# A fused attention and two-layer kernel: another packing of layer two's streamed weight sums

## The chip, the cores and the metric

The kernel runs on one core of one Trainium2 chip. The metric is device time in microseconds, taken over several executions of the whole program; one more execution was recorded by the hardware profiler. The engines are named as in the profile: PE is TensorE (matmuls), PEld its weight loads, DVE is VectorE, ACT is ScalarE, POOL is GpSimd, SP is SyncE, which here issues the DMAs.

## The reference

The inputs are q, k, v of 4 batches x 8 heads x 576 rows x 64, a feature matrix omega, and two weight matrices for each of two layers, all float32. An attention with random features gives 2,304 tokens of 512 channels; two layers 512 to 2048 to 512 follow, the first with a leaky ReLU, the second with a hard swish. The change is in the second.

```
def _moe2_ref(x, w_in, w_out):
    h = x @ w_in                       # 2304 x 512 by 512 x 2048
    relu6 = np.clip(h + 3.0, 0.0, 6.0)
    g = h * relu6 / 6.0
    return (g @ w_out).astype(np.float32)

def reference(**kwargs):
    ...
    attn_out = _attn_ref(**attn_kwargs)
    B, H, S, D = attn_out.shape
    x = np.ascontiguousarray(attn_out.transpose(0, 2, 1, 3)).reshape(B * S, H * D)
    x = _moe_ref(x=x, **moe_kwargs)
    return _moe2_ref(x=x, **moe2_kwargs)
```

## The kernel before

**Products.** A float32 number is split into a rounded high half and the rest, and a product is made of three matmuls (high by high, low by high, high by low). Tokens go in five groups: four of 512 and one of 256; layer two takes them in the order 0, 2, 3, 4, 1. For a group of 512 tokens, layer two cuts its matrices in 2 x 2 blocks and makes seven block products instead of eight (Winograd's form of Strassen). The seven are named b11, b21, t1, t2, t3, t4 and b22. What each multiplies is a block, or a sum of blocks, of x and of the weight.

**Weight sums.** `prepare` (L538 to L578) makes the sums of the weight blocks for one pair of 128-column weight rows, splits each into halves (`split`, L580: a copy and a subtraction, on ACT, DVE or POOL), and stores the result in four parts to DRAM (`away`, L587, the store is L590). This runs during layer one, eight times for w_in. `S[0]` and `S[1]` hold the four sums, `a` and `b` the plain blocks. The list `both` (L566) says which pieces make up which of the four parts.

**Reading.** `Hpair` (L1039 to L1098) makes one pair for a group of 512 tokens: four groups of eight pairs. It fetches the four parts into tiles c[0] to c[3] (`fetch`, L627, issued on SP at L630). The slots of these tiles are a ring of five (`NSUM = 5`), in the profile `late_w` and `third_w`, the latter being one slot of them. Part 2 is fetched only in its first 256 columns, the others in 512. Each of the seven products is six matmuls of 128x256 (L1057), in two banks of PSUM: p takes b11, t2, t3 and t4 in turn, summed on top of each other, and `save` (L1065, an ACT copy of L461) takes a snapshot between them; the two halves of q take b21, and t1 with b22. `total` (L1068) adds a snapshot to a half of q on DVE. So t2, t3 and t4 each wait for the copy that reads the bank before them, and a later b22 for the sum that reads its half. The hard swish follows on ACT and DVE (L1090, L1095).

**After it.** `parts` (L956) sums the blocks of the result (POOL and DVE: L464, L468, L469) and splits them; `down` (L971 to L988) makes seven products of three matmuls (L979) against w_out, which stays in SBUF, into four accumulator banks; `finish` (L990) adds the accumulators on DVE (L1000) and stores the output. For a group that is not stored ahead, the blocks of x are summed and split on the way (`seven`, L608; its subtractions are L464 as well). In the group of 256 tokens `Hsingle` (L1100 to L1125) makes the plain product from the plain blocks in the four parts, with 256-column matmuls (L475 to L477).

**The order.** No order is written by hand. Every operation is handed to `Graph` (L79) with a due time, the tiles that it reads and writes and, for each engine that may run it, an assumed duration. `run` (L154) goes through the operations that are ready and takes the one that can start first by these durations; within 60 ns the earlier due time decides. The slot of a tile is given out in the order in which tiles were asked for. A pair of `Hpair` is due every 7.2 us (`UP`), and its products at these shares of it:

```
prod(0, 0, 0, B_["b11"], 0.0, True)
prod(1, 0, 256, B_["b21"], 0.1, True)
...
prod(2, 1, 0, B_["t1"], 0.2, False)
...
prod(0, 1, 256, B_["t2"], 0.3, False)
```

`down` of a pair is due three pairs later, so that its products and those of `Hpair` alternate on PE. The order that comes out is a fixed program for each engine, with semaphores between them.

## Time and profile before

| what | us |
|---|---|
| median of 3 runs | 915.52 |
| their range | 915.23 to 915.98 |
| profiled execution | 912.86 |
| its span in the trace | 910.8 |
| PE busy | 900.3 |
| layer two, from the first matmul of L1057 | 543.4 to 906.4 |

The span is the time from the first to the last recorded instruction; the profiled execution's own time is 2.1 us more. Some matmul records of a trace can be missing, and the ends of matmuls are modelled: a matmul is written with the time that it takes to pass through the array, while the next starts behind it after less than half of that. So the step between starts is what counts, and in a run of n equal matmuls it is found as (length - one duration) / (n - 1).

### The profile page before, as it was taken

How to read it: one execution, taken by the hardware profiler on the slowest of the kernel's cores; microseconds unless marked ns; L12 is line 12 of the kernel's file. 1: busy time of each engine (PE TensorE's matmuls, PEld its weight loads, DVE VectorE, ACT ScalarE, POOL GpSimd, SP SyncE). 2: the span in 40 equal slices, each digit the busy share in tenths (PEclk: the TensorE clock that was granted, in tenths of full speed). 3: DMA queues.
4: the chain of work that ended last, by engine and by line, in shares of the span. 5: the costliest groups of instructions: out<-in, count | busy, mean ns of one | idle time of the engine just before them, and what ended most of it. 6: DMA issues, size and time to landing. Idle time of an engine off the chain costs nothing.

```text
span 910.8 us, 17874 instructions
## 1 busy us (share of the span) xinstructions
PE 900.3 (99%) x6340; PEld 801.5 (88%) x6340; DVE 614.1 (67%) x1518; ACT 493.3 (54%) x1157; POOL 319.5 (35%) x565
## 2 busy tenths in 40 slices
PE   8999999999999999999999999999999999999998
PEld 8978777889868877788888888999999999999997
DVE  5888987977786774555587444666666557676554
ACT  7966766766676654544555335443543455455442
POOL 2454554422541211101001002344426436544642
PEclk9999999999999999999999999999999999999999
DMA  9537644767567670978998438885787584678540
GB/s 333 156 119 250 208 147 139 229 212 205 164 191 235 207 214 26 333 290 301 323 335 314 143 135 283 308 313 163 238 279 275 172 277 137 219 237 256 163 131 33
DMA packets 91849, 198.01 MB, mean 217 GB/s; under 512 B 15088, under 2 KB 41328, under 8 KB 91760
## 3 DMA queue, kind: packets, MB, share of 16 engines
q1 hardware_dynamic: 91760, 196.87, 65.0%
q8 instruction: 50, 0.82, 0.4%
q14 instruction: 39, 0.32, 0.1%
HBM read 150.18 MB, written 46.66 MB: 216 GB/s over the span
## 4 chain that ended last, share of the span: by engine, by line
PE 91%; DVE 5%; issue 1%; ACT 1%; DMA 1%; POOL 0%; SPq 0%; DVEq 0%; ACTq 0%
PE bank L979 18%; PE bank L1057 17%; PE bank L475 16%; PE bank L477 15%; PE bank L476 15%; PE bank L708 4%; PE bank L754 3%; PE bank L889 1%; PE bank L861 1%; PE bank L765 1%; DVE nm L677 1%; DVE junk L836 1%; DMA first_xT<-qT 1%; DVE sq L655 0%; DVE late_u L1000 0%
## 5 line engine op out<-in xcount | busy, mean ns | idle before, releaser
L979 PE MATMUL bank<-w,g 128*128 128x256 f32 x762 | 108.0, 279 | 0.5 <-DVE g L464 0.4
L979 PEld LDWEIGHTS bank<-w,g 128*128 128x128 f32 x762 | 96.8, 188 | 1.1 <-DVE g L464 0.8
L461 ACT COPY late_u<-bank 128x256 f32<-128x256 f32 (+1 forms) x112 | 43.0, 385 | 93.1 <-PE bank L1057 81.7
L921 DVE TENSOR_TENSOR g<-bank,g 128x512 fp32r<-128x512 f32 (+1 forms) x80 | 50.8, 635 | 56.6 <-ACT g L461 55.4
L919 ACT ACTIVATE bank<-bank 128x512 f32<-128x512 f32 (+1 forms) x80 | 43.7, 546 | 74.8 <-PE bank L477 74.6
L1057 PE MATMUL bank<-x,late_w 128*128 128x256 f32 x552 | 73.8, 280 | 0.7 <-DVE u L1000 0.5
L1057 PEld LDWEIGHTS bank<-x,late_w 128*128 128x128 f32 x552 | 68.0, 188 | 1.3 <-DVE u L1000 0.7
L475 PE MATMUL bank<-g,w 128*128 128x512 f32 (+1 forms) x180 | 68.9, 383 | 0.0
L1057 PE MATMUL bank<-second_w,late_w 128*128 128x256 f32 x498 | 68.3, 280 | 0.5 <-ACT late_u L461 0.5
L475 PE MATMUL bank<-x,w 128*128 128x512 f32 (+1 forms) x180 | 68.6, 381 | 0.0
L477 PE MATMUL bank<-g,w 128*128 128x512 f32 (+1 forms) x180 | 66.4, 369 | 0.0
L477 PE MATMUL bank<-x,w 128*128 128x512 f32 (+1 forms) x180 | 66.3, 368 | 0.0
L476 PE MATMUL bank<-x,w 128*128 128x512 f32 (+1 forms) x180 | 66.2, 368 | 0.0
L476 PE MATMUL bank<-g,w 128*128 128x512 f32 (+1 forms) x180 | 66.2, 368 | 0.0
L683 POOL TENSOR_TENSOR nm<-nm,sq 128x4 f32<-128x4 f32 (+3 forms) x92 | 27.8, 310 | 107.9 <-DVE nm L680 101.7
L677 DVE TENSOR_REDUCE nm<-bank 128x4 f32<-128x512 f32 (+3 forms) x92 | 49.6, 568 | 23.3 <-PE bank L708 20.6
L688 ACT ACTIVATE h<-bank,nm 128x128 f32<-128x128 f32 x208 | 58.7, 387 | 11.4 <-POOL nm L683 11.4
L1057 PEld LDWEIGHTS bank<-second_w,late_w 128*128 128x128 f32 x498 | 62.0, 188 | 1.0 <-ACT late_u L461 0.7
L979 PE MATMUL bank<-second_w,g 128*128 128x256 f32 x333 | 48.2, 278 | 0.0
L475 PE MATMUL bank<-x,second_w 128*128 128x512 f32 (+1 forms) x120 | 45.2, 377 | 0.0
L461 ACT CAST g<-bank 128x512 fp32r<-128x512 f32 (+1 forms) x78 | 43.4, 557 | 1.4
L477 PE MATMUL bank<-x,second_w 128*128 128x512 f32 (+1 forms) x120 | 44.1, 367 | 0.0
(353 smaller groups left out, 2424.4 us busy)
## 6 DMA issues: line engine op xcount, KB each, us to landing
late_w<-in SPq DMA_DIRECT2D x84, 512.0 KB, 4.4
in<-late_w SPq DMA_DIRECT2D x32, 512.0 KB, 4.1
late_w<-in SPq DMA_DIRECT2D x40, 256.0 KB, 4.3
third_w<-in SPq DMA_DIRECT2D x20, 512.0 KB, 4.4
wst<-w2i SPq DMA_DIRECT2D x16, 512.0 KB, 4.2
wst<-w2o SPq DMA_DIRECT2D x16, 512.0 KB, 4.2
x_t<-late_w SPq DMA_DIRECT2D x12, 512.0 KB, 4.4
wst<-w1i SPq DMA_DIRECT2D x10, 512.0 KB, 4.1
```

The lines of the kernel that those rows point to most:

```text
L461: return [("act", c_act(n, psum), lambda: nc.scalar.copy(dst(), src())), dve if psum else dve + (True,)]
L475: nc.tensor.matmul(o, lhsT=ah, rhs=bh, start=start, stop=False)
L476: nc.tensor.matmul(o, lhsT=al, rhs=bh, start=False, stop=False)
L477: nc.tensor.matmul(o, lhsT=ah, rhs=bl, start=False, stop=stop)
L677: g.op([("dve", c_dve(c * 128), lambda raw=raw, n_=n_: nc.vector.tensor_reduce(out=n_()[:, :, 0], in_=raw(), axis=AX.X, op=ALU.min))], rd= ...
L683: ("pool", 170, lambda n_=n_, s_=s_: nc.gpsimd.tensor_tensor(out=n_(), in0=n_(), in1=s_(), op=ALU.subtract))],
L688: nc.scalar.activation(h.tiles[0][:, q * 128:q * 128 + 128], raw()[:, q], AF.Exp, bias=nm.tiles[0][:, q], scale=-1.0)
L708: nc.tensor.matmul(ps[bank].tiles[0][o, i * 128:i * 128 + 128], lhsT=src.tiles[0][r, i * 128:i * 128 + n], rhs=wn[r], start=True, stop=True)
L919: g.op([("act", c_act(n, True), lambda: nc.scalar.activation(P(), P(), AF.Prelu, alpha=0.01))], wr=[p], due=d)
L921: g.op([("dve", c_dve(n), lambda: nc.vector.tensor_tensor(out=G1(), in0=P(), in1=G0().bitcast(F32), op=ALU.subtract))], rd=[p, (gg, 0)], w ...
L979: nc.tensor.matmul(acc[bank].tiles[0][:, half * 256:half * 256 + 256], lhsT=src.tiles[x][:, q * 128:q * 128 + 128], rhs=w[k].tiles[y][:, c ...
L1057: nc.tensor.matmul(R[r](), lhsT=w[x], rhs=m[y], start=start and k == n == 0, stop=k == 1 and n == 2, skip_group_check=True)
```

## The change

The four parts are packed in another way, and read in the order that follows from it. Nothing is added to or taken from the seven products.

| part | before | after |
|---|---|---|
| c0 | b11, b21 | b11, t2 |
| c1 | t1, t2 | b21, t3 |
| c2 | t3 (256 columns fetched) | t1, t4 |
| c3 | t4, b22 | b22 (256 columns fetched) |

The products that read each tile first were b11, t1, t3 and t4; now they are b11, b21, t1 and b22. `prepare` makes every part of two pieces of 256 columns, where two parts were one piece of 512. `Hsingle` fetches its first tile in two pieces.

```diff
--- before.py
+++ after.py
@@ -563,7 +563,7 @@
             add(1, B_[1], P[0], ALU.subtract, [b, (S[0], 0)])
             add(2, B_[1], A[1], ALU.subtract, [a, b])
             add(3, B_[0], P[1], ALU.subtract, [b, (S[0], 1)])
-        both = [(a, 0, 512)], [(S[0], 0, 512)], [(S[1], 0, 256), (b, 0, 256)], [(S[1], 256, 256), (b, 256, 256)]
+        both = [(a, 0, 256), (S[0], 256, 256)], [(a, 256, 256), (S[1], 0, 256)], [(S[0], 0, 256), (b, 256, 256)], [(S[1], 256, 256), (b, 0, 256)]
         if kind == "out":
             if i % 2 == 0:
                 tail.append(Buf("w", line="wo2"))
@@ -1043,7 +1043,7 @@
             d = t0 - 8e3
             c = [Buf("w", line="c") for _ in range(4)]
             for k in range(4):
-                fetch(c[k], "in", i, k, d + UP * 0.1 * k, slice(0, 256) if k == 2 else slice(0, 512))
+                fetch(c[k], "in", i, k, d + UP * 0.1 * k, slice(0, 256) if k == 3 else slice(0, 512))
             p, q = Ps("H"), Ps("H")
             R = [lambda: p.tiles[0][:, 0:256], lambda: q.tiles[0][:, 0:256], lambda: q.tiles[0][:, 256:512]]
             bank = [(p, 0), (q, 0), (q, 1)]
@@ -1070,16 +1070,16 @@
                     rd=[bank[r], (s, i)], wr=[(h, half)], due=t0 + UP * at - 6e3)
 
             prod(0, 0, 0, B_["b11"], 0.0, True)
-            prod(1, 0, 256, B_["b21"], 0.1, True)
+            prod(1, 1, 0, B_["b21"], 0.1, True)
             save(0, 0.1)
-            prod(2, 1, 0, B_["t1"], 0.2, False)
+            prod(2, 2, 0, B_["t1"], 0.2, False)
             total(h0, 0, 1, 0, 0.2)
-            prod(0, 1, 256, B_["t2"], 0.3, False)
+            prod(0, 0, 256, B_["t2"], 0.3, False)
             save(1, 0.3)
-            prod(0, 2, 0, B_["t3"], 0.5, False)
+            prod(0, 1, 256, B_["t3"], 0.5, False)
             save(0, 0.5)
             total(h1, 1, 2, 0, 0.5)
-            prod(0, 3, 256, B_["t4"], 0.6, False)
+            prod(0, 2, 256, B_["t4"], 0.6, False)
             g.op(copy_alts(lambda: h1.tiles[0][:, 0:256], R[0], 256, True), rd=[bank[0]], wr=[(h1, 0)], due=t0 + UP * 0.7 - 6e3)
             prod(2, 3, 0, B_["b22"], 0.8, False)
             total(h0, 1, 2, 1, 0.8)
@@ -1105,8 +1105,8 @@
             ps = []
             for e in range(2):
                 c, p, h = Buf("w", line="c"), Ps("H"), Buf("u", line="h")
-                for part, cols, to in ((2, 256, 0), (3, 256, 256)) if e else ((0, 0, 0),):
-                    fetch(c, "in", i, part, t0 - 8e3, slice(cols, cols + (256 if e else 512)), to)
+                for part, cols, to in ((3, 256, 0), (2, 256, 256)) if e else ((0, 0, 0), (1, 0, 256)):
+                    fetch(c, "in", i, part, t0 - 8e3, slice(cols, cols + 256), to)
                 ps.append(p)
                 P, U = lambda p=p: p.tiles[0][:, 0:n], lambda h=h: h.tiles[0][:, 0:n]
                 for k in range(KT):
```

Since the order is planned, the edit moves more than the lines above say. In the rows below a matmul that waits is written by itself, and the other five of the product in the row behind it. `Activation` is the semaphore of ACT, `DMAHW` with a number one of the DMA queue's, and DVE the one of DVE. In these rows second_w_1 is the x block of t2, second_w_3 (before: second_w_4 and second_w_3) that of t3, x_101 that of t4 and x_102 that of b22; late_w and third_w are the streamed tiles.

PE in steady state, the second half of one pair, before (t2, t3, t4, b22 with products of L979 between them):

```order
L1057 MATMUL bank_185<-second_w_4_0_1004,late_w_3_0_4052 128x256 [waits Activation_49]
L1057 MATMUL bank_185<-second_w_4_0_1004,late_w_3_0_4052 128x256 x5
L979 MATMUL bank_181<-w_100,g_105 128x256 x3
L979 MATMUL bank_186<-w_99,g_105 128x256 x3
L1057 MATMUL bank_185<-second_w_3_0_1003,late_w_1_0_4050 128x256 [waits DMAHW5_49,Activation_49]
L1057 MATMUL bank_185<-second_w_3_0_1003,late_w_1_0_4050 128x256 x5
L979 MATMUL bank_187<-second_w_0_0_1000,g_105 128x256 x3
L979 MATMUL bank_188<-w_98,g_106 128x256 x3
L1057 MATMUL bank_185<-x_101,late_w_0_0_4049 128x256 [waits DMAHW6_49,Activation_49]
L1057 MATMUL bank_185<-x_101,late_w_0_0_4049 128x256 x5
L1057 MATMUL bank_184<-x_102,late_w_0_0_4049 128x256 [waits DVE_49]
L1057 MATMUL bank_184<-x_102,late_w_0_0_4049 128x256 x5
```

The same piece of a pair after:

```order
L1057 MATMUL bank_182<-second_w_1_0_1001,late_w_3_0_4052 128x256 [waits Activation_49]
L1057 MATMUL bank_182<-second_w_1_0_1001,late_w_3_0_4052 128x256 x5
L979 MATMUL bank_183<-w_97,late_g_0_0_4053 128x256 x3
L979 MATMUL bank_187<-w_99,late_g_0_0_4053 128x256 x3
L1057 MATMUL bank_182<-second_w_3_0_1003,late_w_0_0_4049 128x256 [waits Activation_49]
L1057 MATMUL bank_182<-second_w_3_0_1003,late_w_0_0_4049 128x256 x5
L979 MATMUL bank_188<-w_96,g_107 128x256 x3
L979 MATMUL bank_181<-w_96,g_107 128x256 x3
L1057 MATMUL bank_182<-x_101,third_w_0_0_1650 128x256 [waits Activation_49]
L1057 MATMUL bank_182<-x_101,third_w_0_0_1650 128x256 x5
L1057 MATMUL bank_186<-x_102,late_w_1_0_4050 128x256 [waits DMAHW2_49,DVE_49]
L1057 MATMUL bank_186<-x_102,late_w_1_0_4050 128x256 x5
```

The waits for the DMA have moved from t3 and t4 to the first half of the pair and to b22; t2, t3 and t4 keep their wait for Activation.

DVE at the turn from group 3 to group 4, before (L1000 adds the accumulators of `finish`; second_w and x are the split blocks of x for group 4):

```order
L464 TENSOR_TENSOR second_w_4_0_1004<-xr_0_113,second_w_4_0_1004 128x512
L464 TENSOR_TENSOR second_w_3_0_1003<-xr_0_114,second_w_3_0_1003 128x512
L464 TENSOR_TENSOR x_101<-late_xr_1_0_4060,x_101 128x512
L1000 TENSOR_TENSOR u_0_116<-late_u_2_0_4056,bank_181 128x256
L468 TENSOR_TENSOR late_xr_1_0_4060<-late_xr_1_0_4060,xr_0_113 128x512
L1000 TENSOR_TENSOR late_u_2_0_4056<-late_u_2_0_4056,bank_181 128x256
L1000 TENSOR_TENSOR u_0_116<-u_0_116,bank_181 128x256
L1000 TENSOR_TENSOR late_u_2_0_4056<-late_u_2_0_4056,bank_188 128x256
L1000 TENSOR_TENSOR u_0_116<-u_0_116,bank_184 128x256
```

And after:

```order
L464 TENSOR_TENSOR g_105<-xr_0_112,g_105 128x512
L464 TENSOR_TENSOR g_107<-wst_0_109,g_107 128x384
L1000 TENSOR_TENSOR late_u_2_0_4056<-late_u_2_0_4056,bank_181 128x256
L1000 TENSOR_TENSOR late_u_0_0_4054<-late_u_0_0_4054,bank_181 128x256
L1000 TENSOR_TENSOR late_u_2_0_4056<-late_u_2_0_4056,bank_188 128x256
L1000 TENSOR_TENSOR late_u_0_0_4054<-late_u_0_0_4054,bank_184 128x256
L464 TENSOR_TENSOR x_101<-late_xr_1_0_4060,x_101 128x512
L464 TENSOR_TENSOR second_w_1_0_1001<-xr_0_113,second_w_1_0_1001 128x512
L464 TENSOR_TENSOR second_w_3_0_1003<-xr_0_114,second_w_3_0_1003 128x512
```

The four adds of L1000 now stand ahead of the three subtractions of L464 that make blocks of x.

## Rows read from the trace of the kernel before

**Rows 1.** The page: span, busy time of each engine, shares of the last chain.

```profile
span 910.8 us, 17874 instructions
...
PE 900.3 (99%) x6340; PEld 801.5 (88%) x6340; DVE 614.1 (67%) x1518; ACT 493.3 (54%) x1157; POOL 319.5 (35%) x565
...
PE 91%; DVE 5%; issue 1%; ACT 1%; DMA 1%; POOL 0%; SPq 0%; DVEq 0%; ACTq 0%
```

**Rows 2.** Stretches of PE: from:to, length, busy (matmuls), clock, DMA share, GB/s.

```profile
543.40:906.40 363.00, 361.17 (x3074) 1.00 0.67 220
842.00:872.00 30.00, 30.00 (x267) 1.00 0.50 159
836.70:906.40 69.70, 69.39 (x608) 1.00 0.39 122
...
598.60:629.90 31.30, 31.30 (x267) 1.00 0.69 240
...
sum 122.80, PE 122.57; mean PE 12.26
```

**Rows 3.** Timeline from 646.8: start, length, engine, line, operation, count.

```profile
646.81 0.37 ACT L461 COPY late_u<-bank 128x256 f32<-128x256 f32 x1 [1.67 <-PE bank L1057]
...
647.24 0.77 PEld L1057 LDWEIGHTS bank<-second_w,late_w 128*128 128x128 f32 x6
647.29 0.92 PE L1057 MATMUL bank<-second_w,late_w 128*128 128x256 f32 x6
```

**Rows 4.** The timeline again, from 656.0.

```profile
656.02 0.37 ACT L461 COPY late_u<-bank 128x256 f32<-128x256 f32 x1 [1.40 <-PE bank L1057]
...
656.45 1.11 PEld L1057 LDWEIGHTS bank<-x,late_w 128*128 128x128 f32 x9
```

**Rows 5.** Waits of the weight loads in layer two: total us, times, longest.

```profile
PEld bank L1057 <- ACT late_u L461: 1.5, 4, 0.7
PEld bank L979 <- DVE g L464: 0.8, 2, 0.4
PEld bank L1057 <- DVE u L1000: 0.7, 1, 0.7
PEld bank L979 <- ACT late_u L461: 0.5, 2, 0.3
PEld bank L1057 <- DMA late_w<-in: 0.2, 1, 0.2
```

**Rows 6.** Instructions of L1057: count, ns min/median/max, first and last start.

```profile
L1057 PEldq EVENT_SEMAPHORE  x87: 51/51/51, 539.6 to 834.5; - x87
...
L1057 PEld LDWEIGHTS bank<-w,late_w x42: 186/188/192, 543.4 to 595.5; 128*128 128x128 f32 x42
```

**Rows 7.** The same view, of L1068 and of the copies of L461.

```profile
L1068 DVE TENSOR_TENSOR u<-late_u,bank x36: 409/421/423, 546.0 to 816.1; 128x256 f32<-128x256 f32 x36
...
L461 ACT COPY late_u<-bank x112: 363/372/592, 373.7 to 904.3; 128x256 f32<-128x256 f32 x105, 128x512 f32<-128x512 f32 x7
```

**Rows 8.** Timeline of DVE and PE at the turn to group 4.

```profile
771.48 1.82 DVE L464 TENSOR_TENSOR second_w<-xr,second_w 128x512 fp32r<-128x512 f32 x2
...
774.08 0.41 DVE L1000 TENSOR_TENSOR u<-late_u,bank 128x256 f32<-128x256 f32 x1
...
775.81 0.97 PE L1057 MATMUL bank<-x,late_w 128*128 128x256 f32 x6 [0.55 <-DVE u L1000]
```

**Rows 9.** Fetches, L630: count, ns, first and last start; issue to landing.

```profile
L630 SPq DMA_DIRECT2D late_w<-in x124: 319/328/1162, 496.3 to 885.2; - x124
...
DMA to landing us min/median/max: 3.0/4.4/11.5
```

**Rows 10.** Stretches of all engines: the first 27 us of layer two.

```profile
543.40:570.00 26.60, 25.86 (x191) 23.96 (x189) 11.35 (x27) 13.05 (x28) 6.35 (x12) 1.00 0.86 291
```

**Rows 11.** Packing: its stretch, and the stores of L590.

```profile
375.00:443.00 68.00, 68.00 (x302) 56.28 (x301) 39.04 (x88) 32.27 (x73) 5.65 (x6) 1.00 0.86 322
...
L590 SPq DMA_DIRECT2D in<-late_w x32: 319/320/1071, 375.5 to 443.0; - x32
```

## The prediction

> **What bounds the kernel now.** First the busy shares and the chain that ended last [rows 1]: TensorE (PE) is busy for 99% of the span and makes up 91% of the chain. So a gain must either take matmuls away (the change takes none), shorten the step from one matmul to the next, or remove a stall of PE. All code that the change touches at its reading end runs in layer two, so the next view is the table of stretches for PE [rows 2]: from 543.4 us, where the first product of `Hpair` starts, to 906.4 us lie 3074 matmuls in 363.0 us, at a granted clock of 1.00, that is 2.4 GHz, in every row. The clock is not the question.
>
> The same table shows what is: two paces of the same 128x256 matmul. 842.0 to 872.0 holds 267 matmuls in 30.0 us, less the one or two under way at its start: 113.3 ns each. 598.6 to 629.9 holds as many in 31.3 us: 117.7 ns. I call them fast and slow pace; they differ by 4.4 ns. The ten long slow stretches sum to 122.8 us, some 1,043 matmuls. With the short ones between (about 230, followed through the timeline) some 1,280 of the stage's matmuls are slow: 1,280 x 4.4 ns = 5.6 us.
>
> The timeline shows where the pace flips. A ScalarE (ACT) copy out of a bank (`save`, 0.37 us) ran at 646.81, ending at 647.18; the weight load of the next product on that bank began at 647.24, its matmuls at 647.29 [rows 3]. This product starts 6 matmuls (two products of L979) after the copied one, and 6 x 0.113 = 0.68 us do not hold the copy, its latency and the weight load. Without the wait the six matmuls take 0.84 us (five steps of 113.3 ns and a last one of 276); here they take 0.92 us and what follows runs at the slow pace. At 656.02 the same happens the other way round [rows 4]: copy, short wait, and the pace turns fast again. Measured on matmul starts, such a wait costs 53 ns where the pace was fast and 29 ns where it was slow, 41 on average, and each flips the pace. Products whose bank was last used 9 or 12 matmuls before do not wait.
>
> Last the waits of the weight-load engine [rows 5]. Beyond the short waits, which hide in the pipeline there, it names 1.5 and 0.5 us for ACT copies, 0.8 and 0.7 us for DVE, and 0.2 us, once, for a streamed weight.
>
> **The change part by part.**
>
> *Fewer double waits.* A product that waits for two engines has an extra instruction on PE's sequencer for one of them: 87 of them, 51 ns each, of L1057 [rows 6]. In the built order there are 87 such products before and 77 after (DMA with ACT 65 to 7, DMA with DVE 17 to 66, DMA with DMA 5 to 4). The extra instructions stand ahead of the matmuls: the first at 539.6, when the first matmul of L1057 is loaded at 543.4. In the double wait of [rows 4] (the copy and a streamed tile) the weight load began as soon after the copy as in the single wait of [rows 3]. So they are off the path: 0. At most 10 x 51 ns = 0.5 us would be gained.
>
> The Trainium skill ("Perfetto Trace Analysis", Identifying Dependency Chains) says that an instruction that waits on several engines may have event-semaphore instructions put ahead of it; the trace agrees, with 87 of 51 ns. It gives no price on the path.
>
> *Waits for ACT.* The change is to spare the first reader of a tile the wait for ACT. But who waits for ACT is set by the banks: t2, t3 and t4 all go through bank p, and each follows a copy, whichever tile it reads. In the excerpt of PE's order after, t2, t3 and t4 each wait for Activation alone, and two of three stand 6 matmuls behind their bank's last product. Over the whole order there are 42 such products at distance 6 before and 41 after (at 9: 10 and 17; at 12: 22 and 9). So 1 x 41 ns: nothing.
>
> *Waits for DVE.* b22 is now a first reader and waits for the DVE sum (L1068) that empties its bank half. In the order 4 or 5 products stand 6 matmuls behind such a sum that did not before. The sum takes 0.421 us, the copy 0.372 [rows 7]; so each wait costs about 35 to 50 ns more than one for ACT, 62 to 88 ns. Sum +0.3 us (0 to +0.4).
>
> *Pace.* Since each short wait flips the pace, the slow share hangs on where the 41 waits fall and on the parity of what comes before them. Counted on the order of after: if only the waits for ACT at distance 6 flip, 762 matmuls are slow, or, with the other parity, 2,124; if those for DVE flip as well, some 1,400 to 1,490. Before: 1,280. In times: -2.3, +3.7, and +0.5 to +0.9 us. I take the middle, +0.6, since nothing in the trace says that a wait for DVE does not flip, and keep both ends.
>
> The Trainium skill ("TensorE: Matmul & The Clock Gate", Back-to-back issue gap) gives one isolated gap at full clock, columns / 2.4 + 2.5 ns, 109 ns for 256, and says that real spacing comes from weight load and matmul together. By the one gap there would be no second pace, and this term would be 0; the rows show 113.3 and 117.7 ns, so the measurement decides.
>
> *The turn to group 4.* Before, DVE subtracts for the coming group from 771.48 on (two of 1.82 us together, a third behind them), and only then adds the accumulators of L1000, at 774.08 and later [rows 8]. The product at 775.81 waits for these: 0.7 us [rows 5]. In the order of after the four adds stand ahead of the subtractions, as the excerpt of DVE shows. The 0.7 us go; the subtracted tiles are then some 1.6 us later (four adds of 0.41), and their first readers stand further back, so I see no new stall. -0.7 us, from 0 (the stall goes to the next tile) to -1.1 (with part of the 0.8 us for L464 in [rows 5], which lie just ahead).
>
> *Fetches.* Five slots hold the streamed tiles. Before, c0 is read by b11 and b21, c1 by t1 and t2, so a slot comes free after two products. Now c0 goes from b11 to t2, c1 from b21 to t3, c2 from t1 to t4: slots are held longer. Counted from a slot's last reader to the first reader of what is fetched into it, the median falls from 8.8 to 7.7 us (matmuls times the paces above), and margins under 5.6 us rise from 3 to 31; the usual tight one is 43 matmuls, 4.9 us. Against it stand 0.3 us until SyncE issues, and 3.0 to 11.5, at median 4.4 us until it lands [rows 9]: 4.7 us. In steady state it fits barely. In the first group, where DMA engines are busy for 0.86 of the time [rows 10] and other loads are queued ahead on the same queue, it may not. +0.5 us (0 to +1.5).
>
> *Packing.* `prepare` makes its splits in eight pieces of 256 columns per weight row pair instead of two of 512 and four of 256: 16 more copies and 16 more subtractions in all. They run up to the last store at 443.0, beside a PE that is busy for all of the 68.0 us [rows 11]; the first streamed fetch is at 496.3 [rows 9], 53 us later. 0. If this cover were gone, it would be 16 x 0.2 us, 3 us, of ACT. `Hsingle` issues 8 more DMAs of the same bytes in all, in the last 70 us, where the DMA engines stand at 0.39 [rows 2]: 0 (to +0.3, one issue of 0.32 us in the way).
>
> **Sum.** 0 + 0 + 0.3 + 0.6 - 0.7 + 0.5 = +0.7 us. The profiled execution took 912.86 us, 2.1 more than its span of 910.8, and is 2.7 below the median of the runs shown, 915.52; the terms are differences, so I put them on the median: 915.52 + 0.7 = 916.2.
>
> **The rivals.** A measurement of this kernel can tell from no change about 0.2%, 1.8 us.
>
> 1. *The forecast*: the waits stay where the banks put them, the pace share stays about equal, fetches land in time. 914.0 to 917.3. Chance 0.45.
> 2. *Slower, by late fetches.* Place: the first readers of c0 and c1 in the first group, 544 to 600 us, which now find the slot freed only 43 matmuls before. It decides where release to landing is over 4.9 us, and 13 such fetches stand there. At a landing of 4.9 us (half a us above the median) each is some 0.3 us late: +4.0 us, 919.5. For: the 0.86 load of the DMA engines and the 11.5 us of the worst. Against: only 0.2 us was waited for them before, and the queue seems nearly empty when a tight one is issued. Chance 0.15.
> 3. *Slower, by pace.* The parity falls the wrong way: 2,124 slow matmuls, the 605 behind the last `Hpair` among them (before, all of those ran fast: 69.7 us with its waits [rows 2]; slow they cost 605 x 4.4 ns = 2.7 us more). +3.7 us, with the others some 919.2. Chance 0.15.
> 4. *Faster, by pace.* The other parity, 762 slow matmuls, with the turn to group 4: -2.3 - 0.7 to -1.1 = -3.0 to -3.4, 912.3. Chance 0.16.
> 5. *Faster, as the change is meant.* With the first readers free of ACT the short waits vanish: 42 x 41 ns = 1.7 us, and with no flips all runs fast, 5.6 us; with 0.7 for the turn 907.5. Against it: the 41 products at distance 6 that the order still holds. Chance 0.09.
>
> **How the numbers follow.** The likeliest is the forecast, 916.2. Faster: 0.16 + 0.09 = 0.25; same 0.45; slower 0.15 + 0.15 = 0.30. The range leaves out rival 5 and the far ends: 912.0 to 919.8. The forecast's own range is 914.0 to 917.3.
>
> **What would show it.** In the profile after: the extra sequencer instructions at 77 and still ahead of the matmuls; short waits for ACT still at t3 and t4 with 6 matmuls before them, 0.92 us for their six matmuls; the table of stretches with fast and slow at 113.3 and 117.7 ns and a slow share between 1,200 and 1,500; no wait of L1057 for `u` of L1000 near 775; waits for streamed tiles under 1.5 us in all. I am wrong if those waits pass 3 us, if the last 605 matmuls run slow, or if the short waits for ACT are gone.

## The result and the profile after

The changed kernel takes 922.85 us (median of 6 runs, 920.25 to 925.00), the one before 915.70 beside it (6 runs, 914.09 to 915.98). The ratio is 1.0080, with an interval of 1.0062 to 1.0098: 7.2 us slower, where 916.2 and at most 919.8 were predicted. The profiled execution took 924.01 us, 2 us of them outside its span.

The page of after, to be set against [rows 1]: the span, the busy times, and the shares of the chain that ended last.

```profile
span 922.2 us, 17891 instructions
...
PE 906.9 (98%) x6340; PEld 805.7 (87%) x6340; DVE 613.7 (67%) x1527; ACT 494.4 (54%) x1164; POOL 334.5 (36%) x581
...
PE 91%; DVE 4%; DMA 2%; ACT 1%; issue 1%; POOL 0%; DVEq 0%; ACTq 0%; POOLq 0%
```

PE has the same 6340 matmuls, and DMA has gone from 1% of the chain to 2%. POOL has 16 instructions and 15 us more than before; DVE and ACT are as busy as they were. So PE has no more to do than before.

The table of stretches for PE, as in [rows 2]: length, busy time with matmuls, clock, DMA share, GB/s. The first row is all of layer two, the second a piece of it around the turn to group 4, the last two lie in its tail.

```profile
542.20:917.80 375.60, 367.27 (x3073) 1.00 0.65 213
765.00:815.00 50.00, 46.57 (x386) 1.00 0.46 148
844.70:884.20 39.50, 39.50 (x337) 1.00 0.54 170
888.60:915.50 26.90, 26.90 (x230) 1.00 0.24 75
```

Layer two takes 12.6 us more than the 363.0 of before for as many matmuls, at the same granted clock of 1.00. From 765 to 815 it gets 386 matmuls done; the trace of before has 421 in the same stretch. The tail now runs at the slow pace: 337 matmuls, less the one or two under way at the start, in 39.50 us are 117.7 ns each, and it is the same behind the stall at 888. The tail of before ran at 113.3.

A table of the starts of the n-th matmul of layer two, counted in each trace from the stage's first one, shows where the time goes. It gives us behind the trace of before; `before again`, `after again` and `half bytes` are runs told of below.

| matmul of layer two | before, us | before again | after | after again | half bytes |
|---|---|---|---|---|---|
| 420 (end of group 0) | 53.3 | +0.4 | +3.4 | +3.8 | +0.6 |
| 900 | 109.2 | +0.4 | +3.3 | +3.8 | +1.1 |
| 1320 | 157.8 | +0.4 | +6.0 | +4.8 | +1.2 |
| 1820 (ahead of the turn) | 216.6 | +0.4 | +6.0 | +5.2 | +0.9 |
| 2220 (behind the turn) | 264.3 | +0.7 | +10.1 | +8.9 | +4.7 |
| 2790 | 329.7 | +2.4 | +11.8 | +10.6 | +6.6 |
| the last | 362.7 | +2.4 | +12.8 | +11.7 | +6.6 |

Three places take most of it: group 0 (3.4 us), the stretch to matmul 1320 (2.7 in one trace, 1.0 in the other) and the turn to group 4 (some 4). The slow pace of the tail adds 1.6 us up to matmul 2790, as it does in the second trace of before, and 1.0 behind it.

The waits of PE in layer two of after, and, for [rows 5], the largest of the weight loads: engine, line, what was waited for, total us, times, longest.

```profile
PE bank L979 <- DVE g L464: 3.2, 4, 1.2
PE bank L1057 <- DMA third_w<-in: 1.8, 2, 1.3
PE bank L1057 <- DMA late_w<-in: 1.6, 3, 0.7
PE bank L1057 <- DVE u L1068: 0.6, 1, 0.6
...
PEld bank L979 <- DVE g L464: 4.0, 4, 1.4
PEld bank L1057 <- DMA third_w<-in: 2.2, 2, 1.5
```

Before, these weight loads waited 0.8 us for L464 and 0.2 for a streamed tile. The wait of L1057 for `u` of L1000, 0.7 us before, is not among those of after any more; but weight loads of L979 now wait for L1000 in two places, for 0.7 us in all, and at 564.67 PE waits 0.6 us for the sum of L1068, where before has no such wait. Two kinds of stall have grown most: streamed tiles that land late, and halves of `g` (L464) that come late.

**A late tile.** The fetch on SP and its first reader on PE, in group 2: start, length, engine, line, operation, and in brackets the idle time ahead and what ended it.

```profile
665.23 0.32 SPq L630 DMA_DIRECT2D third_w<-in  x1
...
671.49 0.74 PE L1057 MATMUL bank<-w,third_w 128*128 128x256 f32 x4 [1.31 <-DMA third_w<-in]
```

A product whose weights lie in this tile waits for it and goes on 6.3 us after the issue began. Counted in steps between starts it is the largest stall of the trace, 1.48 us above a step at the fast pace. The other four late tiles are read at 558.91, 560.84, 585.71 and 592.84: 0.60, 0.44, 0.85 and 0.79. With the step behind each, which is some 0.1 us long as well, the five make 4.6 us.

**The turn to group 4.** POOL, DVE and PE in the trace of after. L468 and L469 are the same 128x512 step of `parts`, on DVE and on POOL.

```profile
771.38 1.41 POOL L469 TENSOR_TENSOR xr<-xr,xr 128x512 f32<-128x512 f32 x1
...
770.63 0.42 DVE L1000 TENSOR_TENSOR late_u<-late_u,bank 128x256 f32<-128x256 f32 x1 [2.16 <-PE bank L979]
770.97 0.68 DVE L460 CAST late_g<-wst 128x384 fp32r<-128x384 f32 x1
771.57 1.77 DVE L464 TENSOR_TENSOR g<-late_xr,g 128x512 fp32r<-128x512 f32 x1
...
770.35 2.05 PE L979 MATMUL bank<-w,g 128*128 128x256 f32 x16
773.39 0.51 PE L979 MATMUL bank<-w,g 128*128 128x256 f32 x2 [0.99 <-DVE g L464]
```

The planner has given one 128x512 step to POOL that DVE did before. Beside it the subtraction that makes the low half of `g` takes 1.77 us, and PE stands for 0.99 until it is done. In the trace of before this subtraction takes 0.68 us in the same place:

```profile
770.13 0.68 DVE L464 TENSOR_TENSOR g<-xr,g 128x512 fp32r<-128x512 f32 x1
```

The Trainium skill ("GPSIMD Engine Reference", Specifications) says that GpSimd's SBUF interface is shared with VectorE and that the two contend when a VectorE instruction has two SBUF inputs. The trace agrees: 0.68 us become 1.77 with two inputs and a POOL instruction of 1.41 us beside it.

The rows show more than a slowing. POOL's step ends at 771.38 + 1.41 = 772.79, the subtraction 0.55 us later. So it is in all 14 subtractions of 128x512 in layer two of after that begin while a POOL step has more than 0.13 us to run: each ends 0.55 us after that step. The 51 with no POOL step beside them take 0.68 to 0.69 us. Where the subtraction begins first it is POOL that takes longer: beside the line of before, a POOL step of 128x128 takes 0.85 us instead of 0.46. In the second trace of after this happens at the same place: the subtraction begins ahead of POOL's 128x512 step and is held only by the short step before it (771.09 + 0.57 = 771.66); the next one, of 128x384, is held by the long step.

```profile
771.09 0.57 POOL L469 TENSOR_TENSOR late_xr<-wst 128x128 f32<-128x128 f32 x1
771.26 0.94 DVE L464 TENSOR_TENSOR g<-late_xr,g 128x512 fp32r<-128x512 f32 x1
...
771.62 1.73 POOL L469 TENSOR_TENSOR xr<-xr,xr 128x512 f32<-128x512 f32 x1
772.13 1.63 DVE L464 TENSOR_TENSOR late_g<-wst,late_g 128x384 fp32r<-128x384 f32 x1
```

The other two stalls of the turn, at 784.72 and 808.33:

```profile
782.06 0.37 ACT L461 COPY u<-bank 128x256 f32<-128x256 f32 x1 [1.75 <-PE bank L1057]
782.33 0.62 ACT L461 CAST g<-late_xr 128x512 fp32r<-128x512 f32 x1
...
783.11 0.70 DVE L460 CAST x<-late_xr 128x512 fp32r<-128x512 f32 x1
783.73 0.94 DVE L464 TENSOR_TENSOR g<-late_xr,g 128x512 fp32r<-128x512 f32 x1
...
784.72 0.85 PE L979 MATMUL bank<-w,g 128*128 128x256 f32 x5 [1.16 <-DVE g L464]
...
806.61 1.12 POOL L465 TENSOR_TENSOR g<-late_xr,g 128x384 fp32r<-128x384 f32 x1 [2.93 <-DVE g L460]
...
806.78 1.50 DVE L464 TENSOR_TENSOR g<-xr,g 128x512 fp32r<-128x512 f32 x1
...
808.33 0.50 PE L979 MATMUL bank<-w,g 128*128 128x256 f32 x2 [0.82 <-DVE g L464]
```

At 784 the rounded half of `g` (the CAST) stands on ACT behind a copy that waits 1.75 us for PE, and its low half on DVE behind a cast of `x`; both were queued later than what PE needs next. At 808 the subtraction runs beside POOL again, 1.50 us, and ends 0.55 us after POOL's step (806.61 + 1.12 = 807.73). All that PE loses from 765 to 815, in steps over 70 ns above the fast pace, is 5.2 us, against 1.3 before: 3.9 us.

### The profile page after: what moved, and what is told of

It reads as the page before. It is cut to its first block, busy times and chain, and to the rows that moved or that the text cites. A ratio compares the mean times of both kernels' runs of the same rounds, so it can differ in the third digit from the quotient of the medians.

```text
span 922.2 us, 17891 instructions
## 1 busy us (share of the span) xinstructions
PE 906.9 (98%) x6340; PEld 805.7 (87%) x6340; DVE 613.7 (67%) x1527; ACT 494.4 (54%) x1164; POOL 334.5 (36%) x581
## 4 chain that ended last, share of the span: by engine, by line
PE 91%; DVE 4%; DMA 2%; ACT 1%; issue 1%; POOL 0%; DVEq 0%; ACTq 0%; POOLq 0%
PE bank L979 17%; PE bank L475 16%; PE bank L1057 16%; PE bank L477 15%; PE bank L476 15%; PE bank L708 4%; PE bank L754 3%; DMA late_w<-in 2%; PE bank L889 2%; PE bank L861 1%; PE bank L765 1%; DMA third_w<-in 1%; DVE g L464 1%; PE bank L1250 1%; DVE nm L677 0%
## 5 line engine op out<-in xcount | busy, mean ns | idle before, releaser
L979 PE MATMUL bank<-w,g 128*128 128x256 f32 x720 | 102.8, 280 | 3.6 <-DVE g L464 3.2
L979 PEld LDWEIGHTS bank<-w,g 128*128 128x128 f32 x720 | 91.7, 188 | 5.0 <-DVE g L464 4.0
L461 ACT COPY late_u<-bank 128x256 f32<-128x256 f32 (+1 forms) x97 | 37.6, 391 | 87.4 <-PE bank L1057 79.2
L1057 PE MATMUL bank<-x,late_w 128*128 128x256 f32 x546 | 75.2, 281 | 0.8 <-ACT u L461 0.5
L1057 PEld LDWEIGHTS bank<-x,late_w 128*128 128x128 f32 x546 | 68.0, 188 | 1.8 <-ACT late_u L461 0.8
L688 ACT ACTIVATE h<-bank,nm 128x128 f32<-128x128 f32 x208 | 58.8, 386 | 12.9 <-POOL nm L683 12.8
L979 PE MATMUL bank<-second_w,g 128*128 128x256 f32 x375 | 54.1, 280 | 0.0
L1057 PE MATMUL bank<-second_w,late_w 128*128 128x256 f32 x354 | 50.2, 282 | 1.9 <-DMA late_w<-in 1.3
L979 PEld LDWEIGHTS bank<-second_w,g 128*128 128x128 f32 x375 | 48.5, 189 | 0.0
L1057 PEld LDWEIGHTS bank<-second_w,late_w 128*128 128x128 f32 x354 | 44.7, 188 | 2.8 <-DVE wst L1095 0.9
L461 ACT COPY u<-bank 128x256 f32<-128x256 f32 (+1 forms) x53 | 22.1, 423 | 46.0 <-PE bank L1057 40.7
L464 DVE TENSOR_TENSOR g<-late_xr,g 128x512 fp32r<-128x512 f32 (+1 forms) x50 | 37.1, 743 | 12.3 <-ACT g L461 11.7
```

Source lines behind the costliest of these rows:

```text
L461: return [("act", c_act(n, psum), lambda: nc.scalar.copy(dst(), src())), dve if psum else dve + (True,)]
L464: return [("dve", c_dve(n), lambda: nc.vector.tensor_tensor(out=dst(), in0=src(), in1=hi().bitcast(F32), op=ALU.subtract), True), ("pool", ...
L688: nc.scalar.activation(h.tiles[0][:, q * 128:q * 128 + 128], raw()[:, q], AF.Exp, bias=nm.tiles[0][:, q], scale=-1.0)
L979: nc.tensor.matmul(acc[bank].tiles[0][:, half * 256:half * 256 + 256], lhsT=src.tiles[x][:, q * 128:q * 128 + 128], rhs=w[k].tiles[y][:, c ...
L1057: nc.tensor.matmul(R[r](), lhsT=w[x], rhs=m[y], start=start and k == n == 0, stop=k == 1 and n == 2, skip_group_check=True)
```

## The experiments

The planner makes it hard to change one thing: a line that is touched moves hundreds of instructions. So the planned order of all engines was written into the kernels as a table and replayed: which operation comes next on each engine, and which engine does it. With the table of its own kernel this gives the same program as the planner. Packing, order and single instructions can then be changed apart. Ratios are against the kernel before, timed on the same chip.

**Packing and order apart.** The first kernel has the new packing (the diff of the change) with the order of before, the second the old packing with the order of after.

```diff
 order of the engines' work
-planned for this packing
+planned for the other packing
```

> The packing of after, with every engine's instructions in the order that the planner made for before (the products on TensorE stand word for word as before; only which streamed tile a product reads, and the fetches, differ). Theory (the time comes from slots that are held longer, so that a fetch lands after its first reader; the planner of after moved products about to make room for it, and other stalls came with that order): the fetches now stand 13 to 37 matmuls ahead of their readers at a dozen places of the first group, against the 41 or so (4.7 us) that they need, so waits of L1057 for streamed tiles rise to 7 to 12 us and the time to 925 (921 to 930), slower than after. Rival (the packing costs nothing, all comes from the planner's new order): 915.7, as before. Rival (the pace alone): 915.7 too, since the waits for ScalarE stand where they stood, or 918 if the parity falls the wrong way.

Measured: 931.09 us (930.01 to 934.92), ratio 1.0186 (1.0161 to 1.0211), 16.5 us slower.

> The packing of before, with every engine's instructions in the order that the planner made for after. Slots come free after two products again: all but two fetches have 46 matmuls or more between release and first reader. Theory: the waits for streamed tiles (4.2 us in after) go, the stalls at the turn to group 4 behind L464 (3.5 us) and the larger slow share (1,830 matmuls) stay: 918.5 (917 to 920.5); one fetch at the turn to group 4 has 13 matmuls only and may cost up to 3 us there. Rival (all is in the order): 922.8, as after. Rival (all is in the packing): 915.7, as before.

Measured: 922.44 us (921.60 to 924.84), ratio 1.0088 (1.0070 to 1.0106). The waits of the weight loads in the first, then the main ones of PE in the second:

```profile
PEld bank L1057 <- DMA late_w<-in: 11.1, 12, 2.1
PEld bank L1057 <- DMA third_w<-in: 3.2, 4, 1.0
```

```profile
PE bank L1057 <- DMA late_w<-in: 2.2, 1, 2.2
PE bank L979 <- DVE g L464: 1.0, 2, 0.8
PE bank L1057 <- DMA third_w<-in: 0.8, 1, 0.8
```

The packing by itself costs 16.5 us, more than the 5 to 14 that were expected, and 14.3 us of the first kernel's waits of weight loads are for streamed tiles. The new order keeps these waits small with the new packing, and the loss is down to some 7 to 8 us. But the order has a price of its own: with the old packing, which doesn't need it, it is as slow as after. Here the expectation (918.5) missed: it had the waits for streamed tiles gone, and 3.0 us of them are there, 2.2 at the turn to group 4, where one fetch had only 13 matmuls, and 0.8 in group 0. Without these the order would cost nearer 5 us than 8 (an estimate from the two waits). So taking one of the two back would have gained nothing, and their prices do not add.

The two kernels also tell whose loss the turn is. From matmul 1820 to 2220 the old order with the new packing takes 47.9 us, where before has 47.7 and after 51.9; the new order with the old packing takes 53.9, of which 2.2 are the wait for the tile. The loss at the turn comes with the order and not with the packing.

**Fetches.** The program of after, with only the high halves fetched; every instruction stays where it was.

```diff
-b.tiles[2].rearrange(...)[:, :, to:to + n], d[:, :, cols]
+b.tiles[2].rearrange(...)[:, 0:1, to:to + n], d[:, 0:1, cols]
```

> After, same order on every engine, but each fetch of a streamed tile brings only the high halves, half of the bytes; the products read what the slot held before as low halves. Theory (fetches are late because the slot comes free late and the transfer then takes its time): from issue to landing the fetches take under 4 us at the median instead of 4.6, nearly all waits of L1057 for streamed tiles go (3.5 us in after), and the time falls by 3 to 4 us, to 919. Rival (late because of the queue or the wait before the issue, the bytes matter little): median landing stays, waits stay, 922 to 923.

Measured: 919.11 us (918.82 to 919.30), ratio 1.0051 (1.0036 to 1.0065). The time from issue to landing, of after and of this run, and PE's largest waits in this run:

```profile
DMA to landing us min/median/max: 2.9/4.6/11.0
```

```profile
DMA to landing us min/median/max: 2.2/2.8/8.7
...
PE bank L979 <- DVE g L464: 2.1, 3, 1.2
PE bank L1057 <- DVE u L1068: 0.8, 1, 0.8
PE bank L979 <- DVE late_u L1000: 0.6, 2, 0.4
```

No product waits for a streamed tile any more. Steps of 60 to 100 ns over the fast pace at L1057, of which after has 15 (1.2 us), its second trace 13 and before 2, are down to 3, so these too go with the bytes fetched. The table above shows group 0 and the stretch to 1320 without loss (+0.6 and +1.2), while the turn costs what it did. Late tiles are worth 0.3% (1.0080, or 1.0082 for after timed again, against 1.0051), 2.6 to 2.8 us, with an uncertainty of some 2. By the traces it is more: the steps over 70 ns sum to 9.0 us here, 14.9 and 13.6 in the two of after. What remains is 4.3 us above before. In its trace 3.8 us are lost at the turn, which the two kernels above put down to the order; that the order makes all of the 4.3 is not shown.

**The turn.** First the one step of `parts` back on DVE, with PE's order untouched.

```diff
 POOL, then DVE
-L469 TENSOR_TENSOR xr_0_113<-xr_0_115,xr_0_113 128x512
...
 L1000 TENSOR_TENSOR late_u_0_0_4054<-late_u_0_0_4054,bank_181 128x256
+L468 TENSOR_TENSOR xr_0_113<-xr_0_115,xr_0_113 128x512
 L1000 TENSOR_TENSOR late_u_2_0_4056<-late_u_2_0_4056,bank_188 128x256
```

> After, in its own order, with one 128x512 subtraction of the x blocks for group 4 moved from GpSimd (L469, at 771.4) to VectorE (L468). Theory (VectorE's L464 at 771.57 took 1.77 us instead of 0.68 because GpSimd worked beside it, and the product of L979 at 772.1 waited 1.16 us for it): L464 takes 0.7 to 1.0 us there, that stall falls under 0.4, and the time falls by 0.8 us, to 922.0. Rival (L464 is late for another reason, GpSimd has no part in it): its duration stays near 1.8 us and the time at 922.8, or the extra 0.68 us on VectorE shows as a new stall a few us later.

Measured: 922.46 us (921.15 to 925.02), ratio 1.0079 (1.0063 to 1.0096). The subtraction and PE at this place:

```profile
772.25 0.66 POOL L469 TENSOR_TENSOR late_xr<-wst 128x128 f32<-128x128 f32 x1
...
772.51 0.95 DVE L464 TENSOR_TENSOR g<-late_xr,g 128x512 fp32r<-128x512 f32 x1
...
771.64 2.38 PE L979 MATMUL bank<-w,g 128*128 128x256 f32 x18
```

The 18 matmuls now run without a gap; the subtraction waits only for the end of a short POOL step, at 772.91. From matmul 1876 to 1926 PE loses 0.2 us in this trace. In the five that have POOL's step and the same order of PE there (after, after again, half bytes, old packing with the new order, and the first kernel of the pace below) it loses 1.1 to 1.4: at this subtraction, or at what stands behind it on DVE. So the cause of this stall is shown. The time doesn't show it: by the ratios 0.1 us less than after, within the spread. In the trace the matmuls 1820 to 2220 cost 2.6 us where after has 4.1, but the kernel was 0.6 behind after ahead of them, and by matmul 2420 it is 0.2 behind after again, by other stalls.

Then all three places: the step on DVE as above but further ahead, and the casts and subtractions of `g` moved ahead of what waits.

```diff
 DVE
 L464 TENSOR_TENSOR second_w_3_0_1003<-xr_0_114,second_w_3_0_1003 128x512
+L464 TENSOR_TENSOR g_106<-late_xr_0_0_4059,g_106 128x512
 L1068 TENSOR_TENSOR late_u_4_0_4058<-u_0_117,bank_188 128x256
 L468 TENSOR_TENSOR late_xr_1_0_4060<-late_xr_1_0_4060,xr_0_113 128x512
 L460 COPY u_0_116<-bank_181 128x256
 L460 CAST x_102<-late_xr_1_0_4060 128x512
-L464 TENSOR_TENSOR g_106<-late_xr_0_0_4059,g_106 128x512
```

> After, same order on TensorE and SyncE. Around the turn to group 4, one 128x512 subtraction goes from GpSimd to VectorE, and two pairs of splits for products of L979 (a cast on ScalarE, its L464 on VectorE) stand ahead of a copy that waits for TensorE, instead of behind it. Theory (the three stalls of 1.16, 1.32 and 0.99 us for L464 are made by the order of the engines beside TensorE, not by too much work): all three go, 3.3 us less than after on this chip. Rival (ScalarE, VectorE and GpSimd are short of time there, and a wait removed comes back on the next tile): under 1 us less.

Measured: 919.51 us (918.48 to 925.73), ratio 1.0053 (1.0026 to 1.0079). Its seven times lie at two levels, 918.5 to 919.5 and 922.6 to 925.7; its trace is of the upper one, and what sets the level stays open. So the median, 3.7 us under after on this chip, can't be set against the 3.3 that were expected. In that trace the matmuls 1820 to 2220 cost 2.4 us where after has 4.1 and after again 3.7. In place of the three stalls stand smaller ones:

```profile
775.46 2.56 PE L979 MATMUL bank<-w,g 128*128 128x256 f32 x20 [0.43 <-DVE g L464]
...
783.40 0.73 PE L1057 MATMUL bank<-x,third_w 128*128 128x256 f32 x4 [0.21 <-DVE x L464]
...
787.28 0.97 PE L1057 MATMUL bank<-w,late_w 128*128 128x256 f32 x6 [0.43 <-DMA late_w<-in]
```

So the order of DVE, ACT and POOL at the turn is a cause, by 1.3 to 1.7 us of the 4 in this trace; the rest goes to what is late next. Nearly all of that the first edit had brought already.

**The pace.** First the parity at one place: one product of L979 moved ahead of two of L1057 near 844 us, which removes the short wait that flips the pace there in after; and in before a like move, to make the tail slow.

```diff
 PE, near the last pair of Hpair (pace_new)
+L979 MATMUL bank_187<-second_w_0_0_1000,g_106 128x256 x3
 L1057 MATMUL bank_181<-x_102,late_w_3_0_4052 128x256 x6
 L1057 MATMUL bank_184<-x_104,late_w_2_0_4051 128x256 x6
-L979 MATMUL bank_187<-second_w_0_0_1000,g_106 128x256 x3
```

> After, in its own order, with one product of L979 (three matmuls) put ahead of the last t4, which then stands 9 instead of 6 matmuls behind its bank's last product. Theory (a short wait for ScalarE flips the pace, and the flip at 844.5 sets the pace of the last 567 matmuls): the short wait at 844.5 is gone, the matmuls behind it run at 113.3 instead of 117.7 ns, and the time falls by 2.5 us, to 920.3. Rival (the pace is set by something else in that stretch, such as the tiles read or the traffic of the DMA engines): they stay at 117.7 ns and the time falls by the one wait, 0.05 us.

Measured: 920.06 us (920.00 to 923.28), ratio 1.0067 (1.0047 to 1.0086); by the ratios 1.2 us under after, with intervals that overlap. In its trace, of the slowest of the four runs, the short wait is gone, but the pace was slow already from an earlier wait:

```profile
842.80:887.90 45.10, 45.10 (x383) 1.00 0.51 163
```

> Before, in its own order and packing, with one product of L979 put ahead of the last t4 (9 matmuls behind its bank's last product instead of 6). Theory (each short wait flips the pace): the flip from slow to fast at 835.9 is gone, the last 605 matmuls run at 117.7 instead of 113.3 ns, and the kernel gets 2.6 us slower, 917.8, by doing one wait less. Rival (a short wait only costs itself): 0.03 us faster, 915.1.

Measured: 912.82 us (911.21 to 915.35), ratio 1.0000 (0.9984 to 1.0015). In its trace the tail does run slow, up to a stall at 877, and is 1.4 us later for it. But the second trace of before, told of below, has the same slow tail without the edit, and the 2.6 us that were expected don't show in the times. So neither kernel tells what sets the pace of the tail.

Then the short waits themselves. Wherever fewer than nine matmuls stood between two products on one bank, the next product of L979 was moved in between: 74 times in the order of before, 70 in that of after.

```diff
 PE
+L979 MATMUL bank_185<-w_84,late_g_0_0_4053 128x256 x3
 L1057 MATMUL bank_181<-second_w_3_0_1003,late_w_3_0_4052 128x256 x6
-L979 MATMUL bank_185<-w_84,late_g_0_0_4053 128x256 x3
```

> Before, same packing, same order on every engine but TensorE; there 74 products of L979 move ahead of a t3 or t4, so that nearly all of these stand 9 matmuls behind their bank's last product (one wait at 6 is left, in the first pairs). Theory (short waits cost 1.9 us themselves, and their flips 5.7 us of slow pace): hardly a short wait is left, long stretches keep one pace, mostly the fast one, which follows the larger stalls; 908.5 (907 to 911). Rival (pace does not come from the waits): 1.5 us less at most, 913.5, with as many slow matmuls as before, 1,280. Rival (the moved products come before their inputs are ready): new waits of L979 for L464 of some us, 915 or more.

> The same for after: its packing and its order, with 70 products of L979 moved ahead of t2, t3 or t4. Theory: the slow pace (8.2 us in after) and the short waits (1.6 us) mostly go, late fetches (some 4 us) and the stalls at the turn to group 4 (some 4 us) stay; 914.5 (913 to 917). Rival (what after loses is all pace): as the same edit of before, 908.5. Rival (pace does not come from the waits): 921.5.

Measured: 910.80 us (909.06 to 913.85), ratio 0.9983 (0.9966 to 1.0000), and 919.54 us (918.11 to 921.18), ratio 1.0073 (1.0045 to 1.0100). The steps above the fast pace, sorted by size in the traces, tell what happened: up to 9 ns each they are the pace, from 9 to 70 short waits, above that stalls.

| layer two, us | pace | short waits | stalls |
|---|---|---|---|
| before | 5.7 | 2.0 | 4.3 |
| before again | 7.5 | 2.0 | 4.9 |
| after | 8.2 | 1.6 | 14.9 |
| after again | 8.4 | 1.6 | 13.6 |
| half bytes | 7.8 | 1.8 | 9.0 |
| new packing, old order | 6.5 | 1.9 | 22.5 |
| old packing, new order | 7.3 | 1.6 | 13.4 |
| spread, on before | 4.4 | 0.3 | 8.3 |
| spread, on after | 2.9 | 0.5 | 14.6 |
| spread and turn, on before | 7.8 | 0.35 | 6.8 |

The short waits can be taken away, 1.7 us on before. The moved products make stalls of their own (4.3 to 8.3), and where few waits are left one pace lasts longer, the slow one too. On before it nets a gain of 2.0 us by the medians, 1.6 by the ratio, where some 7 were expected, at the edge of what can be told: the one kernel with a ratio under 1. On after the expected 914.5 was missed as well; by the ratios it gains 0.6 us, within the spread.

A last version, 4 us under before by its expectation, was to keep that gain and take the stall of [rows 8] away: the four adds of L1000 ahead of the subtractions for group 4, as in after, with POOL left alone.

```diff
 DVE, at the turn to group 4
-L464 TENSOR_TENSOR second_w_4_0_1004<-xr_0_113,second_w_4_0_1004 128x512
-L464 TENSOR_TENSOR second_w_3_0_1003<-xr_0_114,second_w_3_0_1003 128x512
-L464 TENSOR_TENSOR x_101<-late_xr_1_0_4060,x_101 128x512
 L1000 TENSOR_TENSOR u_0_116<-u_0_116,bank_181 128x256
 L1000 TENSOR_TENSOR late_u_2_0_4056<-late_u_2_0_4056,bank_188 128x256
 L1000 TENSOR_TENSOR u_0_116<-u_0_116,bank_184 128x256
+L464 TENSOR_TENSOR second_w_4_0_1004<-xr_0_113,second_w_4_0_1004 128x512
+L464 TENSOR_TENSOR second_w_3_0_1003<-xr_0_114,second_w_3_0_1003 128x512
+L464 TENSOR_TENSOR x_101<-late_xr_1_0_4060,x_101 128x512
```

> Before's packing, with 67 products of L979 moved ahead of t3 or t4 as in the earlier kernel of that kind, but none whose accumulator or input comes later than that place, and on VectorE the four adds of L1000 ahead of the subtractions of x at the turn to group 4, one L464 ahead of a cast. Theory: the new waits for L1000 that the earlier kernel had (2.5 us in its trace) go, so does the 0.7 us wait near 775; the slow pace falls to under 4 us: 4 us less than before on this chip (3 to 7). Rival (each removed wait comes back elsewhere): 2 us less, as the earlier one.

Measured: 915.72 us (913.89 to 916.97), ratio 1.0000 (0.9988 to 1.0012). Two stretches of PE, and the turn:

```profile
607.10:694.90 87.80, 87.80 (x747) 1.00 0.75 260
727.00:766.30 39.30, 39.30 (x336) 1.00 0.75 239
```

```profile
775.35 1.28 DVE L464 TENSOR_TENSOR second_w<-xr,second_w 128x512 fp32r<-128x512 f32 x2
...
776.09 0.74 PE L1057 MATMUL bank<-second_w,late_w 128*128 128x256 f32 x4 [1.09 <-DVE second_w L464]
```

747 and 336 matmuls at 117.7 ns: the pace stuck slow, 7.8 us in all. One step of 142 ns, at 648.71, stands in the middle of the 747 and leaves it slow. And the move that spared 0.7 us of waiting for L1000 made PE wait 1.09 us for the first subtracted block.

**The same programs again.**

> The kernel after, unchanged, on this chip, so that the next two can be compared with it and with before: 7 us slower than before by every theory; in its trace the same stalls at the turn to group 4 (L464, 1.0 to 1.3 us each, three of them), while late fetches may fall on other tiles.

Measured: 923.21 us (922.59 to 923.77), ratio 1.0082 (1.0065 to 1.0099), 7.8 us slower. Of the three stalls two are there as before, steps 1.31 and 0.99 us above the fast pace at 784.53 and 808.01; the first is split in three, of which the largest is 0.52. The late tiles fell elsewhere, as expected: 1.53 and 1.28 us in group 0, and the one in group 2 that cost 1.48 in the first trace lands in time.

> The kernel before, unchanged, for a second trace of it. Theory (waits in layer two are fixed by the order, so the pace flips at the same products in each execution): the slow share is within 30 matmuls of 1,280 and the last 605 are fast; what the first trace had less than the median of its runs (2.7 us) stands in layer one or outside of the span. Rival (the parity falls otherwise from run to run): another slow share, some hundreds of matmuls away.

Measured: 915.23 us, with a span of 913.2 us, where the first trace of before has 910.8. Layer two, and its tail up to and behind the stall at 877:

```profile
543.60:908.80 365.20, 362.76 (x3073) 1.00 0.66 219
837.10:876.30 39.20, 39.20 (x335) 1.00 0.51 164
877.20:908.70 31.50, 31.19 (x273) 1.00 0.24 72
```

The same program on another execution: here 335 matmuls of the tail, less one or two, take 39.20 us, 117.5 ns each; then it is fast. In [rows 2] all 608 matmuls of the tail are fast. Counted as steps of 116 to 122 ns between starts, 1,668 matmuls of layer two are slow here, against 1,256 in the first trace (1,280 in the prediction): the rival held. Set against this trace, the second trace of after is 8.8 us longer in span: 8.7 by stalls, 0.9 by pace, and 0.4 less by short waits, with small differences in layer one. That is near the 7.8 of the medians on its chip; the 11.4 between the two first traces were too much because that of before was a quick one and that of after a slow one.

## Why the prediction was wrong

**The turn to group 4 failed most.** The step read: the adds of L1000 stand ahead, the 0.7 us go, the first readers of the subtracted tiles stand further back, no new stall; -0.7 us. The adds did move and the wait of L1057 for them is gone (a weight load of L979 waits 0.4 us for another L1000 there), but the turn costs 3.9 us more: the term is wrong in sign, by 4.6. It rested on one excerpt of DVE and on one consumer. Not looked at were POOL, which had been given a 128x512 step that holds up DVE's subtraction beside it, 1.77 us instead of 0.68, and the halves of `g` that the same DVE and ACT make for L979, which moved back behind work that waits for PE. Even the part that was looked at was judged wrongly: in the last kernel the same move, made together with the products of L979, spared 0.7 us and left a wait of 1.09 for the first subtracted block, a case outside the term's upper bound of 0. The crossed kernels put the loss at the turn down to the order; the edits of the order took back 1.3 to 1.7 us of it in their traces, and why the rest comes back on the next tiles stays open.

**Fetches.** The mechanism was named twice, as a term (+0.5, up to 1.5) and as rival 2 (+4.0, chance 0.15). Rival 2 was right in kind. PE waits 3.4 us for streamed tiles in after, more than the 3 that stood as a sign of being wrong. The rival's size was near: 4.6 to 5.9 us by the traces, 2.6 to 2.8 by the times of the half fetch. Of its places half were right: four late tiles lie in group 0, and not 13, and one in group 2, where the margin was taken to fit barely. The step that failed is the comparison of a margin of 4.9 us with the median landing of 4.4 plus 0.3: with 31 margins under 5.6 us, it is the landings above the median that count (the tile in group 2 was some 6 us on its way), and the chance that some of 31 are late is not small. Nor did the prediction ask what the planner had already paid for its margins; with the old order the new packing has 14.3 us of waits for tiles.

**Pace.** There are two paces in every trace, and a change of pace that lasts stands at most seven steps behind a step over 122 ns. The step that failed is "each flips the pace". In before it holds: 40 of 40 short waits flip it, and 40 of 41 in its second trace (waits of 9 to 70 ns, those within seven steps of each other taken as one, and the pace read from the steps ahead of it and behind it). In after 15 of 25 do, and 18 of 26 in its second trace; the others leave the pace as it was, most of them steps of 141 to 145 ns in a slow stretch. So no count by parity (762, 1,400 to 1,490 or 2,124) could come out: 1,814 and 1,846 matmuls are slow in the two traces. Why a short wait flips the pace in one place and not in another stays open.

The term of +0.6: the pace costs 8.2 and 8.4 us in the traces of after, 5.7 and 7.5 in those of before. Against the second of before the term nearly holds; its base doesn't: 1,280 slow matmuls were taken as a property of the program, and the same program had 1,668 in another execution. For the same reason the last 605 matmuls at the slow pace, put down as a sign against the forecast, came, and mean little: they are slow up to the stall at 877 in a trace of before too. And the profiled time of before, 2.7 us under its median, should have said so.

**Waits for DVE.** +0.3 us, as four or five short ones. The short steps of this size at L1057 (15 in after) go down to 3 when the fetches are halved, so most of them were late tiles. What DVE did add is one wait at the start of the stage, for a sum of L1068: 0.6 us in after, 0.8 with half the bytes, none in before. Its size is above the term's upper end of 0.4; PE's waits for ACT in group 0 are about as long as before (0.6 us, after 0.5).

**Right.** Double waits: 77 of them, off the path:

```profile
L1057 PEldq EVENT_SEMAPHORE  x77: 51/51/312, 540.9 to 844.4; - x77
```

Waits for ACT: they stay where the banks put them, 1.6 us of short waits against 2.0. The gain that the change is meant for, a first reader without ACT, is at most these 0.4 us. Packing in layer one: 0; the first weight load of L1057 is at 542.0 against 543.4 in [rows 6], and the start of layer two varies by as much between executions of one program.

**Sum.** Of the 7.2 us, late tiles make some 3 and the turn some 4; the wait for DVE in group 0 makes at most 0.6, the double waits and layer one nothing that can be seen; the pace and the spread of an execution blur each by a us or two. What stays open: what decides at which parity an execution falls, why single traces spread by 2 us, and the two levels of the turn kernel. The prediction's largest fault was to give 0.45 to a sum of small terms, when, by the two tables of the order, 109 of PE's 1,592 operations and some 130 of DVE's 1,316 stand in another place, and they had been followed at two.

## What to carry to other kernels

When a planner sets the order, look at every engine at the places where the old order waited, above all at what has been handed from one engine to another, before a stall is counted as removed. A slot that is held longer is paid by the slowest landings and not by the median one, so weigh each tight margin against the spread of the landings. Where a time is set by which of two paces an engine falls into, take it from several traces of the same program before it goes into a sum.

## What the runs showed of the hardware

- The same program runs with its matmuls of 256 columns at 113.3 or 117.7 ns in different places from one execution to another: 1,256 and 1,668 slow ones in two traces of before, with 910.8 and 913.2 us of span.
- One pace can last long: up to 408 fast and 392 slow matmuls in a row without a longer step (the two spread kernels on before). A lasting change stands at most seven steps behind a step over 122 ns, but not each such wait changes it: 40 of 40 short ones in before, 15 of 25 in after.
- A stall costs more than the long step: the step behind it is longer as well, by about 0.11 us in most cases (221 to 223 ns instead of 113.3).
- A VectorE subtraction of 128x512 with two SBUF inputs takes 0.68 to 0.69 us with no GpSimd step beside it. If it begins while GpSimd is at a step, it ends 0.55 us after the end of that step: 0.95 us in all where the step had 0.40 left, 1.50 where it had 0.95, 1.77 where it had 1.22. If VectorE begins first, it takes its 0.68 us and the GpSimd step is the longer one (0.85 instead of 0.46 us for 128x128).
- Half the bytes in a fetch bring its median landing from 4.6 us to 2.8.
